# Fixed probability tiles, declared independences and a moved memset in a two-branch attention kernel

## The chip, the core and the metric

The kernel runs on one core of one Trainium2 chip. The metric is the device time of one execution in microseconds (us), as a median of repeated executions. The engines of a core have instruction queues of their own and meet only at semaphores: PE multiplies matrices (PEld is its weight load), DVE reduces and adds, ACT computes exponentials and copies, POOL computes on SBUF tiles, and SP issues most of the DMAs.

## What is computed

The reference runs two attentions over the same input `x` (2048 tokens, 448 features, 16 heads of 28) and mixes them with a gate per token. Branch A looks back over eight positions with a stride of two; branch B is full attention.

```python
g = _sigmoid((x * gate_w).sum(-1, keepdims=True))
# A: logits over idx = pos - 2*[0..7], softmax, weighted sum, @ A_wo
# B: scores = einsum("bhqd,bhkd->bhqk", q, k) * Dh**-0.5
#    o = einsum("bhqk,bhkd->bhqd", softmax(scores), v);  o @ B_wo
return g * a + (1 - g) * b
```

Everything is fp32. Products that need the precision are made of a high and a low part (`QH`, `QL`, `KH`, `KL`), three matmuls for one.

## The kernel before, in words

**Stages.** Up to about 259 us the kernel projects `x` to queries, keys and values; the inputs stand in four pairs of SBUF blocks `xh`, `xl` (pool `xp`, lines 205 and 206) and the results pass through a pool `pp` of eight slots of 4 KB a partition (lines 46 and 86). Then come 256 steps (the loop at line 1034): 16 units `u` (four groups of four heads, by four blocks of 512 queries) by 16 key tiles `kt`. The last twenty or so steps also carry the output projection, and the rest of it follows.

**One step.** `scores` (line 987) issues the matmuls of one key tile in a fixed order of tokens, `WITH` (line 979):

```python
WITH = "10 20 s0 11 21 30 00 12 22 31 01 s1 s2 32 02".split()
```

A token such as `12` is head "1", term 2 of three; heads 1 and 2 share the two banks of `RP[0]` (tile T2), heads 3 and 0 the two banks of `mine`. `s0`, `s1` and `s2` are matmuls of another kind: they compute, for a unit further on, scores whose row maxima are wanted (line 143). `s0` goes to the bank `T1`, `s1` and `s2` to the two banks of `other`. `mine` and `other` are `RP[1]` and `TP` (tiles T0 and T1) and change places each step (line 995).

As soon as `22` is out, ACT takes the exponential of both banks of `RP[0]` (line 1014, "the first exp"), and after `02` that of `mine` ("the second exp"); each writes a tile P of 128 by 1024. DVE takes the maxima of the extra matmuls (line 147): that of `s0` alone, and a second one over `s1` and `s2` together ("the wide reduce", 128x2 from 128x1024). At the end of the step come the eight matmuls of P with the values of the step before (`do_av`, line 973).

The first token of the next step needs `RP[0]` read by the first exp. `s1` needs `other` read by the second exp of the step before. `30` and `00` need `mine`, which was `other` one step earlier, read by the wide reduce of the step before. After step 234 the extra matmuls are finished, and the order `ALONE` (line 980) holds.

**What sets the order.** Each engine's queue is written out by hand: `at` (line 521) hangs a call on a step and a position in it ("pre", "mid", "dve", "act", "end"), and `issue` (line 717) takes the items of branch A from lists by keys, costs and lags in steps. Branch A runs on POOL (multiplications and additions, lines 608 to 663) with its reductions on DVE (line 618). POOL also has a part of finishing each unit: `fin_on` (line 880) multiplies the unit's sum, and ACT (`fin_hi`, line 884) then rounds it, at the position "pre" of a step, ahead of that step's exps in ACT's queue.

**Semaphores.** The framework derives the dependences from the tiles that instructions touch. A tile taken from a pool slot waits for all who used the slot before. Two readers of one PSUM bank on different engines are put in order as well. An instruction carries one wait of its own; where it has more, they stand ahead of it in the queue of its engine as EVENT_SEMAPHORE records. `tc.declare_no_dep` takes a single dependence out. The kernel before uses it only for the banks of the output projection (line 554).

**Memory.** `pp` stays for the whole kernel: its eight slots hold staging tiles in the projection and P afterwards. When the projection ends, `mp` (line 561) takes the space where `xp` lay, with `KH2`, `KL1`, `maskt` and two more; `pm` (line 567, eight tiles of 2 KB for `mtile`) follows. `init_kh(KH[2])` (line 566) sets KH2 to one in POOL's queue, ahead of the memsets of `maskt`; the DMAs that load its keys are issued at step 12 (line 574), and its first use is unit 8.

Of the kernel before, what the change touches and what calls it, by code (L numbers as in the profile page):

```python
# [8 lines left out]
F32 = mybir.dt.float32  # L9
F32R = mybir.dt.float32r  # L10
AF = mybir.ActivationFunctionType
ALU = mybir.AluOpType
X = mybir.AxisListType.X
ET = mybir.EngineType

S, D, H, DH = 2048, 448, 16, 28
# [3 lines left out]
SCALE = DH ** -0.5  # L20
NU = NG * NB
NMX = 192
# [3 lines left out]
def gated_mix_kernel(ctx: ExitStack, tc: tile.TileContext, xT, xn, gw, wA, wB, woAB, out):  # L26
    nc = tc.nc
# [15 lines left out]

    cp = ctx.enter_context(tc.tile_pool(name="cp", bufs=1))
    sp = ctx.enter_context(tc.tile_pool(name="sp", bufs=2))
    pp = ctx.enter_context(tc.tile_pool(name="pp", bufs=8))

# [6 lines left out]
    def banks(n):  # L56
        for i in range(n):
            pool = ctx.enter_context(tc.tile_pool(name=f"t{i}", bufs=1, space=bass.MemoryType.PSUM))
            T.append(pool.tile([128, 2, 512], F32, name=f"T{i}"))
# [12 lines left out]
    KH = [cp.tile([128, S], F32R, name=f"KH{i}") for i in range(2)]  # L72
    KL = [cp.tile([128, S], F32R, name="KL0")]
    MX = cp.tile([128, NMX], F32, name="MX")
# [7 lines left out]
    def init_kh(t):  # L82
        nc.gpsimd.memset(t.bitcast(F32), 1.0)

    def pair(name):
        return pp.tile([128, 2, 512], F32, tag="P", name=name)
# [50 lines left out]
    def s1_mm(n, bank, half=False):  # L137
        u, i = divmod(n, 64)
        qs, kc, h = i // 16, i // 4 % 4, i % 4
        if i == 0 and u + 1 < NU:  # L140
            load_qhi(u + 1)
        r = slice(64 * (h // 2), 64 * (h // 2) + 64) if half else slice(32 * h, 32 * h + DH)
        nc.tensor.matmul(bank, qhis[u][h % 2][r, 128 * qs:128 * qs + 128],  # L143
                         KH[u // NB % 3][r, 512 * kc:512 * kc + 512], start=True, stop=True)

    def s1_max(n, k, bank):
        nc.vector.tensor_reduce(MX[:, n % NMX:n % NMX + k], bank, axis=X, op=ALU.max)  # L147
        if n // 64 != (n + k) // 64:
            finished.append(n // 64)
        s1c[0] = n + k  # L150


    def s1_half(k, half):
# [28 lines left out]
    def max_turn(t):  # L182
        r = sp.tile([128, 32], F32, name="nms")
        nc.vector.transpose(r, t)
        return r
# [18 lines left out]
    with tc.tile_pool(name="xp", bufs=1) as xp, tc.tile_pool(name="wp", bufs=2) as wp:  # L204
# [203 lines left out]
        r, t = xst[:, 0, 0:3, :], xst[:, 0, 3, :]  # L408
# [7 lines left out]
        for kt in range(3):  # L416
            nc.vector.tensor_tensor(out=xl[0][:, kt, :], in0=r[:, kt, :], in1=xh[0][:, kt, :].bitcast(F32),
                                    op=ALU.subtract)
        nc.vector.tensor_tensor(out=tail[64:128], in0=t[64:128], in1=tail[64:128].bitcast(F32), op=ALU.subtract)
        nc.vector.tensor_tensor(out=wl0[:, 3, 0:256], in0=wt0[:, 0:256], in1=wh0[:, 3, 0:256].bitcast(F32),  # L420
                                op=ALU.subtract)
# [27 lines left out]
        for n, t in enumerate(tiles):  # L449
# [4 lines left out]
            for w in splits:  # L454
                i, k = (n - splits[w][0]) * splits[w][1], splits[w][1]
# [44 lines left out]
            if n == 64:  # L500
                gate = []
                for sgn, dst in ((-1.0, g_t), (1.0, omg)):
                    e = sp.tile([128, NJ], F32, name="ez")
# [5 lines left out]
            if n == 70:  # L509
                r = max_turn(omw)  # L510
# [10 lines left out]
    def at(pos, st, f):  # L521
        hooks.setdefault((st, pos), []).append(f)
# [4 lines left out]


    tctx[0].close()
    banks(3)  # L530
    RP = T[2], T[0]
    TP = T[1]
# [28 lines left out]
    mp = ctx.enter_context(tc.tile_pool(name="mp", bufs=1))  # L561


    KH.append(mp.tile([128, S], F32R, name="KH2"))
    KL.append(mp.tile([128, S], F32R, name="KL1"))
    init_kh(KH[2])
    pm = ctx.enter_context(tc.tile_pool(name="pm", bufs=8))

    def mtile(name):
        return pm.tile([128, 512], F32, tag="M", name=name)  # L570

    maskt = mp.tile([128, W, NJ, 2], F32, name="maskt")
    nc.gpsimd.memset(maskt, 0.0)
    for st, g, t, src in ((12, 2, KH[2], qk_hi), (30, 1, KL[1], qk_lo), (72, 2, KL[0], qk_lo),
                          (100, 3, KH[0], qk_hi), (136, 3, KL[1], qk_lo)):
# [107 lines left out]
    for c in range(8):  # L683
# [20 lines left out]
        n = 0  # L704
# [197 lines left out]
    for u in range(NU - 1):  # L902
        f = NJ * (u + 1)
# [76 lines left out]
    ALONE = "10 20 30 00 11 21 31 01 12 22 32 02".split()  # L980
    turn = [0]
    order = []

    def sums(i):
        return pbank[2 if i else 1]

    def scores(u, kt, cur):
        g = u // NB
        n = s1c[0]
        k = min(3, s1e - n)  # L990
        qh, ql = Qs[u]
        ks = slice(128 * kt, 128 * kt + 128)
        mine, other = ((RP[1], TP) if turn[0] == 0 else (TP, RP[1]))
        if k:
            turn[0] = 1 - turn[0]
        bank = {"1": RP[0][:, 0, :], "2": RP[0][:, 1, :], "3": mine[:, 0, :], "0": mine[:, 1, :],
                "s0": T1, "s1": other[:, 0, :], "s2": other[:, 1, :]}
        for tok in WITH if k else ALONE:
            if tok[0] == "s":
                i = int(tok[1])  # L1000
                if i < k:
                    s1_mm(n + i, bank[tok])
                if i == 0:
                    s1_max(n, 1, T1)
                elif i == 2 and k > 1:
                    s1_max(n + 1, k - 1, other[:, 0:k - 1, :])
                continue
            a, t = tok[0], int(tok[1])
            h = (int(a) + n) % 4
            r = slice(32 * h, 32 * h + (DH + 2 if t == 0 else DH))  # L1010
            nc.tensor.matmul(bank[a], (KH[g % 3], KH[g % 3], KL[g % 2])[t][r, ks], (qh, ql, qh)[t][r, :], start=(t == 0), stop=(t == 2))  # L1011
            if t == 2 and a in "20":
                p = pair("P")
                nc.scalar.activation(p, RP[0] if a == "2" else mine, AF.Exp, scale=SCALE)  # L1014
                cur[(h + 3) % 4], cur[h] = p[:, 0, :], p[:, 1, :]
                yield len(cur)

# [16 lines left out]
    for u in range(NU):  # L1034
        g, b = divmod(u, NB)
        for kt in range(NJ):
# [12 lines left out]
            for a in scores(u, kt, cur):  # L1049
                if a == 2:  # L1050
                    run("mid", st)
# [45 lines left out]
    for j in range(12, 16):  # L1097
# [4 lines left out]
        bank = acc[j - 12]  # L1102
# [40 lines left out]
```

## Time and profile before

| | |
|---|---|
| median of 3 executions | 927.08 us (926.46 to 927.43) |
| the profiled execution | 927.55 us; span of its instructions 925.1 us |
| granted TensorE clock | 0.996 |
| PE, DVE, ACT, POOL busy | 914.6, 732.6, 652.8, 620.9 us |
| the 512 exps, line 1014 | 497.1 us, mean 1024 ns |
| the 470 reduces, line 147 | 443.4 us, mean 954 ns |
| first and last reduce of line 147 start at | 260.0 and 797.9 us |

The profile is read thus: a group row gives engine, operation, tiles and count, then busy time, mean time of one, and idle time before with what ended it. A timeline row gives start, time, engine, line, operation, tiles, count, and in brackets how long the engine had been idle and who released it. "PEld T L1011 <- ACT P L1014" in the table of waits reads: the weight load of line 1011 was idle until the ACT instruction of line 1014 released it. PE's times overlap, since matmuls are pipelined and run side by side on separate rows of the array, so that PE counts as busy almost always. A q behind an engine's name (ACTq, DVEq) is its sequencer, where the EVENT_SEMAPHORE records run.

### The profile page before, as it was taken

Reading aid. Unit: us, or ns where it says so; the run is one execution under the profiler, and the core shown is the slowest. Engines: PE = TensorE matmul, PEld = TensorE weight load, DVE = VectorE, ACT = ScalarE, POOL = GpSimd, SP = SyncE. Lnnn points to the kernel's source line nnn. Section 1 sums busy time; section 2 is a strip of 40 time slices with the busy share of each in tenths; the row PEclk is TensorE's granted clock in tenths of the full one; section 3 lists DMA queues with packets and bytes.
Section 4 is the critical chain, followed back from the end, with each engine's and each line's share of the span. In section 5 each row is a group of like instructions: output and inputs, shape, how many; then the busy total and the mean of one; then the engine's idle time right before and its main releaser. Section 6 shows DMA issues by size and latency. Waiting matters only on the chain.

```text
span 925.1 us, 21392 instructions
## 1 busy us (share of the span) xinstructions
PE 914.6 (99%) x8396; PEld 541.3 (59%) x8396; DVE 732.6 (79%) x977; ACT 652.8 (71%) x802; POOL 620.9 (67%) x485
## 2 busy tenths in 40 slices
PE   9899999999999999999999999999999999999998
PEld 6688999999954444444444444444444444466667
DVE  6388999999979999999999999999998888500012
ACT  6346534343378888888888888888989889855551
POOL 2289856464469799999999999999994851300100
PEclk9899999999999999999999999999999999999999
DMA  9867603444362341335135232421412123553422
GB/s 254 283 191 219 185 11 82 130 121 128 104 240 64 99 123 46 88 103 130 41 96 151 85 101 63 139 74 30 107 42 53 33 60 99 149 156 112 137 83 98
DMA packets 101124, 104.34 MB, mean 113 GB/s; under 512 B 61652, under 2 KB 71252, under 8 KB 100240
## 3 DMA queue, kind: packets, MB, share of 16 engines
q1 hardware_dynamic: 100880, 102.72, 39.2%
q8 instruction: 65, 1.06, 0.5%
q10 hardware_dynamic: 144, 0.26, 0.2%
q14 instruction: 35, 0.29, 0.1%
HBM read 61.99 MB, written 40.48 MB: 111 GB/s over the span
## 4 chain that ended last, share of the span: by engine, by line
PE 94%; DMA 2%; ACT 1%; SPq 1%; issue 0%; DVE 0%; POOL 0%; ACTq 0%; DVEq 0%; POOLq 0%
PE T L1011 30%; PE av L973 26%; PE r L296 15%; PE T L812 8%; PE r L291 7%; PE r L143 4%; PE T L143 4%; ACT P L1014 1%; PE T L790 1%; DMA V<-in_xT 1%; DMA onlo<-on_lo 1%; DMA qk_hi<-qkh 0%; DMA KH<-qk_hi 0%; SPq L100 0%; SPq L851 0%
## 5 line engine op out<-in xcount | busy, mean ns | idle before, releaser
L1014 ACT ACTIVATE P<-T 128x1024 f32<-128x1024 f32 x512 | 497.1, 1024 | 89.5 <-PE T L1011 87.6
L147 DVE TENSOR_REDUCE MX<-T 128x1 f32<-128x512 f32 x470 | 443.4, 954 | 39.6 <-PE T L143 15.7
L973 PE MATMUL av<-P,V 128*32 128x512 f32 x2048 | 272.8, 605 | 0.0
L1011 PEld LDWEIGHTS T<-QH,KH 30*128 30x128 f32 x1024 | 90.9, 181 | 228.9 <-ACT P L1014 198.5
L143 PE MATMUL T<-KH,QP 28*128 28x512 f32 x704 | 222.0, 461 | 0.1
L1011 PE MATMUL T<-QH,KH 30*128 30x512 f32 x1024 | 220.6, 491 | 1.4 <-ACT P L1014 1.3
L160 DVE TENSOR_REDUCE MX<-r 128x2 f32<-128x1024 f32 x160 | 192.5, 1221 | 29.4 <-PE r L143 24.7
L1011 PE MATMUL T<-QH,KL 28*128 28x512 f32 x1024 | 189.0, 393 | 0.0
L1011 PE MATMUL T<-QL,KH 28*128 28x512 f32 x1024 | 187.4, 392 | 0.0
L608 POOL TENSOR_TENSOR prod<-qt,kt 128x896 f32<-128x896 f32 x64 | 135.1, 2115 | 4.7 <-DMA kt<-a_scr 4.7
L360 ACT ACTIVATE raw<-r 128x896 f32<-128x896 f32 (+1 forms) x64 | 58.9, 921 | 96.7 <-PE r L296 96.7
L663 POOL TENSOR_TENSOR oat<-oat,prod 128x896 f32<-128x896 f32 x56 | 118.1, 2109 | 2.4
L143 PE MATMUL r<-KH,QP 64*128 64x512 f32 x320 | 99.4, 395 | 3.3 <-DMA KH<-qk_hi 3.2
L143 PEld LDWEIGHTS T<-KH,QP 28*128 28x128 f32 x704 | 86.0, 181 | 23.7 <-ACT P L1014 13.9
L658 POOL TENSOR_TENSOR prod<-vt,L 128x896 f32<-128x896 f32 x56 | 95.5, 1705 | 0.5
L361 POOL TENSOR_TENSOR ast<-raw 128x448 f32<-128x448 f32 x48 | 55.5, 1156 | 57.8 <-ACT raw L360 49.2
L1011 PEld LDWEIGHTS T<-QL,KH 28*128 28x128 f32 x1024 | 92.5, 184 | 0.0
L1011 PEld LDWEIGHTS T<-QH,KL 28*128 28x128 f32 x1024 | 91.8, 183 | 0.9
L296 PE MATMUL r<-wh,xh 64*128 64x448 f32 (+1 forms) x512 | 87.8, 363 | 0.0
L973 PEld LDWEIGHTS av<-P,V 128*32 128x32 f32 x2048 | 40.3, 108 | 78.9 <-issue 73.9
L800 DVE TENSOR_TENSOR oalo<-T,oah 128x384 fp32r<-128x384 f32 x16 | 8.9, 557 | 90.9 <-ACT onhi L799 82.3
L296 PE MATMUL r<-wh,xl 64*128 64x448 f32 (+1 forms) x384 | 70.9, 363 | 0.0
(110 smaller groups left out, 1158.5 us busy)
## 6 DMA issues: line engine op xcount, KB each, us to landing
a_scr<-ast SPq DMA_DIRECT2D x24, 448.0 KB
qk_hi<-qkh SPq DMA_DIRECT2D x24, 256.0 KB
qk_lo<-qkh SPq DMA_DIRECT2D x24, 256.0 KB
rbc<-rs SPq DMA_DIRECT2D x60, 64.0 KB
QP<-qk_hi SPq DMA_DIRECT2D x64, 56.0 KB
KL<-qk_lo SPq DMA_DIRECT2D x16, 224.0 KB
QH<-qk_hi SPq DMA_DIRECT2D x64, 56.0 KB
QL<-qk_lo SPq DMA_DIRECT2D x64, 56.0 KB
```

What stands on the lines that cost most here:

```text
L143: nc.tensor.matmul(bank, qhis[u][h % 2][r, 128 * qs:128 * qs + 128], KH[u // NB % 3][r, 512 * kc:512 * kc + 512], start=True, stop=True)
L147: nc.vector.tensor_reduce(MX[:, n % NMX:n % NMX + k], bank, axis=X, op=ALU.max)
L160: nc.vector.tensor_reduce(m, PM[k], axis=X, op=ALU.max)
L291: nc.tensor.matmul(bank, ws[c][rows, k, t[4]:t[4] + 128], x, start=first, stop=last)
L296: nc.tensor.matmul(bank[:, 0:cols], x, ws[c][rows, k, 0:cols], start=first, stop=last)
L608: nc.gpsimd.tensor_tensor(out=p, in0=qt[c], in1=kvt["k", c % 2][:, HALO - DIL * w:HALO - DIL * w + NJ, :], op=ALU.mult)
L658: nc.gpsimd.tensor_tensor(out=dst.rearrange("p j (h d) -> p j h d", d=DH), in0=kvt["v", c % 2][:, HALO - DIL * w:HALO - DIL * w + NJ, :].r ...
L663: nc.gpsimd.tensor_tensor(out=oat[c], in0=oat[c], in1=oat[c, w], op=ALU.add)
L812: writes(bank, nc.tensor.matmul(bank[:, :D], src, wo[c][:, k, :], start=(first and k == ks[0] and i == 0), stop=(last and k == ks[-1] and ...
L973: nc.tensor.matmul(av[32 * h:32 * h + 32, :], V[:, kt, 4 * g + h, :], tiles_[h], start=(kt == 0), stop=(kt == NJ - 1), skip_group_check=True)
L1011: nc.tensor.matmul(bank[a], (KH[g % 3], KH[g % 3], KL[g % 2])[t][r, ks], (qh, ql, qh)[t][r, :], start=(t == 0), stop=(t == 2))
L1014: nc.scalar.activation(p, RP[0] if a == "2" else mine, AF.Exp, scale=SCALE)
```

## The change

P is no longer taken from the pool `pp` but from eight fixed tiles `probs`, used in turn, in a new pool `ep`. `pp` is closed with the projection; `pm` takes the first half of its space, `KL1` and `KH2` lie in the second half, and the eight tiles come to lie where the `x` blocks lay. The dependence of an exp on the exp that wrote the same tile eight exps earlier is declared away. So is that between successive readers of the two banks that change places: the wide reduce no longer waits for the second exp that read them before it, nor the second exp for the wide reduce. The matmuls that write the tiles or banks in between keep their waits. KH2's memset moves from the start of the attention to the end of step 2 (the third step).

```diff
-    pp = ctx.enter_context(tc.tile_pool(name="pp", bufs=8))
+    pctx = ExitStack()
+    pp = pctx.enter_context(tc.tile_pool(name="pp", bufs=8))
...
     def s1_max(n, k, bank):
-        nc.vector.tensor_reduce(MX[:, n % NMX:n % NMX + k], bank, axis=X, op=ALU.max)
+        r = nc.vector.tensor_reduce(MX[:, n % NMX:n % NMX + k], bank, axis=X, op=ALU.max)
...
+        return r.ins
...
     tctx[0].close()
+    pctx.close()
+    pm = ctx.enter_context(tc.tile_pool(name="pm", bufs=8))
...
+    KL.append(mp.tile([128, S], F32R, name="KL1"))
     KH.append(mp.tile([128, S], F32R, name="KH2"))
-    KL.append(mp.tile([128, S], F32R, name="KL1"))
-    init_kh(KH[2])
-    pm = ctx.enter_context(tc.tile_pool(name="pm", bufs=8))
+    at("end", 2, lambda: init_kh(KH[2]))
...
+    ep = ctx.enter_context(tc.tile_pool(name="ep", bufs=1))
+    probs = [ep.tile([128, 2, 512], F32, name=f"P{i}") for i in range(8)]
...
+    exps = []
+    reader = {}
+
+    def apart(inst, bank):
+        if id(bank) in reader:
+            tc.declare_no_dep(inst, reader[id(bank)], reason="the matmuls between them waited for it")
+        reader[id(bank)] = inst
...
                 elif i == 2 and k > 1:
-                    s1_max(n + 1, k - 1, other[:, 0:k - 1, :])
+                    r = s1_max(n + 1, k - 1, other[:, 0:k - 1, :])
+                    apart(r, other)
...
             if t == 2 and a in "20":
-                p = pair("P")
-                nc.scalar.activation(p, RP[0] if a == "2" else mine, AF.Exp, scale=SCALE)
+                p = probs[len(exps) % 8]
+                e = nc.scalar.activation(p, RP[0] if a == "2" else mine, AF.Exp, scale=SCALE).ins
+                if len(exps) >= 8:
+                    tc.declare_no_dep(e, exps[-8], reason="the matmuls that read it came between")
+                exps.append(e)
+                if a == "0":
+                    apart(e, mine)
```

## The prediction

> **What bounds the kernel now.** I read the page's busy times first, then the table of waits, then the timeline of a few steps in the middle.
>
> ```profile
> span 925.1 us, 21392 instructions
> PE 914.6 (99%) x8396; PEld 541.3 (59%) x8396; DVE 732.6 (79%) x977; ACT 652.8 (71%) x802; POOL 620.9 (67%) x485
> ```
>
> ```profile
> PEld T L1011 <- ACT P L1014: 198.5, 236, 1.1
> ACT P L1014 <- PE T L1011: 87.6, 203, 2.5
> PEld T L1011 <- DVE MX L147: 12.0, 69, 0.5
> POOL prod L608 <- DMA kt<-a_scr: 4.7, 1, 4.7
> POOL L L624 <- DVE L L618: 2.4, 1, 2.4
> ```
>
> PE counts as busy 99% of the span, yet ACT waits for PE at 203 exps and PE's loads wait for ACT at 236 and for DVE at 69. That is a ring in which each waits for the other, and no engine alone sets the pace. To find the ring I follow one chain through three steps, by starts:
>
> ```profile
> 521.18 0.19 PEld L1011 LDWEIGHTS T<-QH,KH 30*128 30x128 f32 x2 [0.84 <-ACT P L1014]
> ...
> 522.25 1.94 ACT L1014 ACTIVATE P<-T 128x1024 f32<-128x1024 f32 x2 [0.41 <-PE T L1011]
> ...
> 524.24 0.18 PEld L143 LDWEIGHTS T<-KH,QP 28*128 28x128 f32 x2 [0.15 <-ACT P L1014]
> ...
> 524.86 1.23 DVE L147 TENSOR_REDUCE MX<-T 128x2 f32<-128x1024 f32 x1 [0.26 <-PE T L1011]
> ...
> 526.13 0.18 PEld L1011 LDWEIGHTS T<-QH,KH 30*128 30x128 f32 x2 [0.15 <-DVE MX L147]
> ...
> 527.03 0.16 PEld L973 LDWEIGHTS av<-P,V 128*32 128x32 f32 x8 [0.36 <-issue]
> ...
> 528.02 0.19 PEld L1011 LDWEIGHTS T<-QH,KH 30*128 30x128 f32 x2 [0.84 <-ACT P L1014]
> ```
>
> A step begins at 521.18. Its two exps start 1.07 later and end at 524.19. That frees `other` for `s1` and `s2` of the next step, loaded at 524.24 (0.05 later). The wide reduce of these starts at 524.86 (0.62) and ends at 526.09 (1.23). This frees the bank of `30` in the step after, loaded at 526.13 (0.04). The matmuls with V follow at 527.03 (0.90), and the next step begins at 528.02 (0.99). The links are 1.07 + 1.94 + 0.05 + 0.62 + 1.23 + 0.04 + 0.90 + 0.99 = 6.84 us for three steps, 2.28 us a step. Over the whole attention:
>
> ```profile
> L147 DVE TENSOR_REDUCE MX<-T x470: 634/699/1229, 260.0 to 797.9; 128x1 f32<-128x512 f32 x79, 128x2 f32<-128x1024 f32 x78
> L147 DVEq EVENT_SEMAPHORE  x234: 21/21/21, 261.0 to 795.6; - x117
> ```
>
> 470 reduces at two a step are 235 steps, so that 234 intervals lie between 260.0 and 797.9: 2.30 us each. The ring of three steps explains 2.28 of 2.30. Two shorter rings lie below it. In one the first exp alone goes back to the next step: 1.07 + 1.02 + 0.05 = 2.14. In the other `s1` leads straight to the V matmuls (the second exp's end at 524.19 lets `s1` load at 524.24, and the first row below shows 0.45 from there): (1.07 + 1.94 + 0.05 + 0.45 + 0.99) / 2 = 2.25.
>
> ```profile
> 524.69 0.16 PEld L973 LDWEIGHTS av<-P,V 128*32 128x32 f32 x8 [0.26 <-issue]
> ```
>
> **The waits declared away.** The row of 234 DVE records above, one for each wide reduce but one, and the row of ACT below show how the second wait is paid for:
>
> ```profile
> L1014 ACTq EVENT_SEMAPHORE  x490: 17/17/924, 259.5 to 894.9; - x164
> L1014 ACT ACTIVATE P<-T x512: 1013/1024/1068, 260.5 to 895.8; 128x1024 f32<-128x1024 f32 x171
> ```
>
> 490 records stand before 512 exps. By the code the first exp has two waits, the matmul `22` and the exp that used its P slot before; so has the second, `02` and the wide reduce before it; and so has the wide reduce, `s2` and the exp before it. In each pair the second wait is old by the time the first ends, but the instruction leaves its queue only after the record. What a record costs is seen in the tail of the attention, where some exps have none. Both of these steps have the same matmuls in front:
>
> ```profile
> 836.54 0.51 PE L1011 MATMUL T<-QH,KH 30*128 30x512 f32 x4
> ...
> 837.55 1.94 ACT L1014 ACTIVATE P<-T 128x1024 f32<-128x1024 f32 x2 [0.97 <-PE T L1011]
> ...
> 850.97 0.51 PE L1011 MATMUL T<-QH,KH 30*128 30x512 f32 x4
> ...
> 852.05 1.94 ACT L1014 ACTIVATE P<-T 128x1024 f32<-128x1024 f32 x2 [2.53 <-PE T L1011]
> ```
>
> ```profile
> L1014 ACTq EVENT_SEMAPHORE  x2: 17/17/17, 852.0 to 852.1; - x2
> ```
>
> The last row is line 1014 in the window 850.5 to 853; in 836.5 to 839 there is no such row. From the first matmul to the exp it is 1.01 us without the record and 1.08 with it: 0.07 us, or 0.017 if only the record's own time counted. I take 0.065. The second exp's record runs under the first exp and costs nothing as long as the exps follow each other (1.94 for both in the rows above); its going gains nothing. For DVE I compare the reduce of `s0`, which has a single wait, with the wide one:
>
> ```profile
> 523.34 0.49 PE L143 MATMUL T<-KH,QP 28*128 28x512 f32 x1
> ...
> 523.91 0.69 DVE L147 TENSOR_REDUCE MX<-T 128x1 f32<-128x512 f32 x1 [0.17 <-PE T L143]
> ...
> 524.24 0.50 PE L143 MATMUL T<-KH,QP 28*128 28x512 f32 x2
> ```
>
> The first matmul ends at 523.83 and its reduce starts 0.08 later; the pair ends at 524.74 and the wide reduce starts 0.12 later. The record costs 0.04 by this, 0.021 by its own time, and as much as on ACT (0.07) at most. I take 0.04. No lengthening is possible from the removal itself, since each instruction keeps the wait that ends last.
>
> Each of the two lies once in the ring of three steps: (0.065 + 0.04) / 3 = 0.035 us a step, which leaves 2.245, as the ring through `s1` goes down by 0.065 / 2 to 2.22 and stays below. Times 234 steps: 8.2 us. By the ends it is (0.017 + 0.021) / 3 x 234 = 3.0 us and (0.07 + 0.07) / 3 x 234 = 10.9 us. In the steps of the tail PE works on the output projection while the exps wait (0.97 and 2.53 us above); nothing is gained there.
>
> The Trainium skill speaks against the DVE half. "VectorE: DVE Perf Modes", in the sections "The DRAIN you can't avoid" and "Rules for kernel authors", says that between chained DVE operations the semaphores cost nothing and only the number of operations counts. By this rule the 0.04 would be zero; no run here yet separates the two.
>
> **What a faster step meets: POOL.** From the end of branch A's start-up to its last unit:
>
> ```profile
> 311.20:703.00 391.80, 391.60 (x3927) 161.81 (x3923) 371.75 (x562) 343.89 (x386) 382.65 (x257) 1.00 0.32 86
> ```
>
> ```profile
> POOL nmt L179 <- ACT nmv L178: 5.3, 3, 4.1
> POOL finv L842 <- DVE finv L841: 1.0, 2, 0.6
> POOL lr L646 <- DVE lr L642: 1.0, 2, 0.6
> ```
>
> ```profile
> 475.35 1.29 POOL L880 TENSOR_TENSOR on<-osb,rbc 128x512 f32<-128x512 f32 x1
> ...
> 478.09 0.63 ACT L884 ACTIVATE onhi<-on 128x512 fp32r<-128x512 f32 x1
> ```
>
> In these 391.8 us (171 steps of 2.29) POOL is busy 382.65, and all that it waits is 1.0 + 1.0 + 5.3, of which 4.1 lies at the edge: 3.2 us. POOL's work doesn't shrink. Its instructions are bound to steps, so that POOL falls behind PE by what PE gains there, 171 x 0.035 = 6.0 us, less the 3.2 that it needn't idle any more: 2.8 us. Behind it stands ACT's rounding of `on`, at the head of a step and ahead of its exps. In the pair above it starts 1.45 us after POOL is done (475.35 + 1.29 = 476.64). Once POOL is that late, ACT waits, and PE behind it. So the window can give 3.2 + 1.45 = 4.65 rather than 6.0, and I take 1.3 us off. The 63 steps outside give their 2.2 us. Net: 6.9 us.
>
> **Tiles and memory.** ACT never waited for POOL or a DMA at line 1014 (its wait by far is the 87.6 for PE), so P's old slots cost no time and the new place gains none. The first exps then overwrite blocks that projection matmuls read, and PE runs those ahead of the exp's own matmul. I cost it at zero.
>
> **KH2's fill.**
>
> ```profile
> L83 POOL MEMSET KH<- x3: 1805/1805/1812, 1.3 to 261.6; 128x2048 f32 x3
> ```
>
> The memset, 1.8 us from 261.6, is covered by POOL's idle 4.7 us before its first product, which waits for a DMA. Moved behind step 2 it still comes ahead of that product, but waits for the last staging tiles in its new place. Late by the whole 1.8 us it would move branch A's start; then the 2.4 us that POOL idles at line 624 take it up. Its loads at step 12 on SP come much later. Zero either way.
>
> **Rivals.** (1) *Only the exp's record matters*, as the skill's rule has it: 0.065 / 3 x 234 = 5.1 us, 3.7 of it in POOL's window, below 4.65, so all of it stays: 922.0. For it: the DVE difference is 0.04 us between matmuls whose ends are modelled. Against it: DVE waits for PE there in most steps, so the record lies behind the wait. (2) *POOL holds the window entirely*: it is late from the start, none of its idle time or slack is to be had, and only the 63 steps outside gain 2.2 us: 924.9. For it: 382.65 of 391.8. Against: the 1.45 us is measured. (3) *The change doesn't remove the records*: the tiles bring another second wait, or the framework joins the dependences otherwise. No change, 927. (4) *Slower*: exps that write P in its new place take longer. Both lie one after the other in the ring, so x longer costs 2x / 3 in each of 234 steps, 156x. It eats the 6.9 us at x = 0.044 and makes the kernel slower by 0.2% from x = 0.056; with x = 0.07 it gives 931. Against it: over all eight old slots the exps take 1013 to 1068 ns with a median of 1024, so that the place of a tile shows little.
>
> **How the numbers follow.** The sum is made on the profiled execution: 927.55 - 6.9 = 920.65. The median shown is 0.47 below it, so I forecast 927.08 - 6.9 = 920.2. Chances: forecast 0.62, (1) 0.15, (2) 0.10, (3) 0.08, (4) 0.05. The range takes in (1) and the bounds of the record's cost: at the lower end 3.0 us, all inside POOL's allowance, 924.1; at the upper end 10.9 us where POOL's lag costs little, about 917.0 after 0.8 us of it. About 0.2% (1.9 us, 925.2) is what a measurement here can tell from no change. Forecast, (1) and (2) are faster by more: 0.87; (3) is the same, 0.08; (4) slower, 0.05.
>
> **What would show it.** Right: line 1014 and the wide reduce have almost no EVENT_SEMAPHORE records; the reduces of line 147 cover about 8 us less from first to last; from a step's first load to its exp there are 1.00 to 1.01 us instead of 1.07; POOL's waits between 311 and 703 shrink, and ACT shows waits of some tenths at line 884 for line 880. Steps in the tail keep their length. Wrong: the records are there; or they are gone and the interval stays at 2.30; or the exps are longer than 1024 ns; or DVE's line 618 or ACT's line 884 waits for POOL by several us.

## The result and the profile after

The changed kernel takes 919.14 us (median of 5, 918.6 to 920.1) against 927.08 before (median of 5, 926.46 to 929.9). The ratio is 0.9908 with a 95% interval of 0.9895 to 0.9921: 7.9 us less, faster by more than the 0.2% that can be told. The profiled execution took 918.6 us with a span of 916.7 us.

First the groups of line 148 (147 before) and of line 1027 (1014 before) in the changed kernel: count, minimum, median and maximum in ns, first and last start in us.

```profile
L148 DVE TENSOR_REDUCE MX<-T x470: 631/699/1235, 258.8 to 789.5; 128x1 f32<-128x512 f32 x79, 128x2 f32<-128x1024 f32 x78
L148 DVEq EVENT_SEMAPHORE  x1: 21/21/21, 259.8 to 259.8; - x1
```

```profile
L1027 ACT ACTIVATE P<-T x512: 1007/1024/1149, 259.2 to 887.3; 128x1024 f32<-128x1024 f32 x171
L1027 ACTq EVENT_SEMAPHORE  x3: 17/17/17, 258.3 to 262.1; - x3
```

The records are gone: 1 instead of 234 at the reduces, 3 instead of 490 at the exps. The work itself takes as long as before (medians 699 and 1024 ns). The reduces now cover 530.7 us from first to last instead of 537.9. So 7.2 us of the 8.4 by which the spans differ come from the attention; 1.2 us lie ahead of it, since the first reduce starts at 258.8 instead of 260.0. That part isn't the change's: in the other runs of the changed code the first reduce starts between 258.6 and 261.0 us, with the same code ahead of it (the last section says what goes with this). From the last reduce to the end of the span it is 127.2 us in both kernels, so that the tail is as long as before.

The chain through three steps, in the timeline of the changed kernel:

```profile
482.43 0.18 PEld L1024 LDWEIGHTS T<-QH,KH 30*128 30x128 f32 x2 [0.84 <-ACT P L1027]
...
483.45 1.94 ACT L1027 ACTIVATE P<-T 128x1024 f32<-128x1024 f32 x2 [0.38 <-PE T L1024]
...
485.44 0.18 PEld L144 LDWEIGHTS T<-KH,QP 28*128 28x128 f32 x2 [0.18 <-ACT P L1027]
...
485.99 1.22 DVE L148 TENSOR_REDUCE MX<-T 128x2 f32<-128x1024 f32 x1 [0.15 <-PE T L1024]
...
487.26 0.18 PEld L1024 LDWEIGHTS T<-QH,KH 30*128 30x128 f32 x2
...
488.17 0.16 PEld L978 LDWEIGHTS av<-P,V 128*32 128x32 f32 x8 [0.37 <-issue]
...
489.17 0.18 PEld L1024 LDWEIGHTS T<-QH,KH 30*128 30x128 f32 x2 [0.84 <-ACT P L1027]
```

1.02 + 1.94 + 0.05 + 0.55 + 1.22 + 0.05 + 0.91 + 1.00 = 6.74 us for three steps, 2.25 a step. Two links are shorter than before: from the first load to the exp 1.02 instead of 1.07, from the load of `s1` to the wide reduce 0.55 instead of 0.62. The load of `30` has no bracket any more, because PEld stood idle for only 0.09 us before it and waits under 0.15 us aren't listed. It still starts 0.05 us after the wide reduce ends, here and in 225 of the 227 steps from 6 to 232, so the ring is closed as before.

Two steps are clearly longer than before: from first load to first load step 79 takes 2.93 us (2.17 before), step 159 takes 3.38 (2.36). Their rows in the changed kernel:

```profile
439.55 0.49 PE L1024 MATMUL T<-QH,KH 30*128 30x512 f32 x2 [0.74 <-DMA QH<-nm]
```

```profile
618.24 1.30 POOL L885 TENSOR_TENSOR on<-osb,rbc 128x512 f32<-128x512 f32 x1
...
619.58 0.63 ACT L889 ACTIVATE onhi<-on 128x512 fp32r<-128x512 f32 x1 [1.03 <-POOL on L885]
```

The first matmul of step 80 waits 0.74 us for the queries of the new unit. In step 159 ACT waits 1.03 us for POOL's product, with that step's exps behind it. Before, neither wait existed. The last two DMAs of those queries were issued at these times, in the kernel before and in the changed one:

```profile
439.73 1.07 SPq L100 DMA_DIRECT2D QH<-nm  x2
```

```profile
436.96 1.07 SPq L101 DMA_DIRECT2D QH<-nm  x2
```

Step 79 begins at 440.92 before, 1.19 us after that issue, and at 436.59 in the changed kernel, 0.37 us ahead of it.

### The profile page after: what moved, and what is told of

It reads as the page before. It is cut to its first block, busy times and chain, and to the rows that moved or that the text cites. A ratio compares the mean times of both kernels' runs of the same rounds, so it can differ in the third digit from the quotient of the medians.

```text
span 916.7 us, 20680 instructions
## 1 busy us (share of the span) xinstructions
PE 904.7 (99%) x8396; PEld 539.3 (59%) x8396; DVE 731.4 (80%) x977; ACT 652.1 (71%) x802; POOL 620.9 (68%) x485
## 4 chain that ended last, share of the span: by engine, by line
PE 80%; POOL 11%; DMA 3%; SPq 2%; ACT 2%; issue 1%; DVE 0%; POOLq 0%; ACTq 0%; DVEq 0%
PE T L1024 22%; PE av L978 20%; PE r L298 15%; PE T L817 8%; PE r L293 7%; PE r L144 4%; POOL prod L613 3%; POOL oat L668 3%; PE T L144 3%; POOL prod L663 2%; SPq L101 2%; ACT P L1027 1%; PE T L795 1%; DMA KL<-qk_lo 1%; DMA V<-in_xT 1%
## 5 line engine op out<-in xcount | busy, mean ns | idle before, releaser
L1027 ACT ACTIVATE P<-T 128x1024 f32<-128x1024 f32 x512 | 497.4, 1025 | 81.0 <-PE T L1024 79.6
L144 PE MATMUL T<-KH,QP 28*128 28x512 f32 x704 | 219.6, 454 | 0.1
L1024 PE MATMUL T<-QH,KH 30*128 30x512 f32 x1024 | 211.2, 489 | 3.0 <-ACT P L1027 2.0
L1024 PE MATMUL T<-QH,KL 28*128 28x512 f32 x1024 | 185.7, 395 | 0.0
L1024 PE MATMUL T<-QL,KH 28*128 28x512 f32 x1024 | 183.5, 392 | 0.0
```

Of the source, the lines that this page charges most:

```text
L1027: e = nc.scalar.activation(p, RP[0] if a == "2" else mine, AF.Exp, scale=SCALE).ins
```

## The experiments

All are edits of the changed kernel, compared with the kernel before on the same chip. Since the start of the attention shifts by some 2 us from run to run, the column "reduces" gives the time from the first to the last start of the reduce's group, as above.

| run | median us | ratio to before (95%) | reduces us |
|---|---|---|---|
| before | 927.08 | | 537.9 |
| the change | 919.14 | 0.9908 (0.9895 to 0.9921) | 530.7 |
| e1_tiles_only | 927.17 | 0.9995 (0.9981 to 1.0009) | 537.8 |
| e2_exp_only | 922.15 | 0.9936 (0.9917 to 0.9955) | 533.6 |
| e3_reduce_only | 922.16 | 0.9941 (0.9920 to 0.9963) | 533.2 |
| e4_second_exp_keeps | 920.22 | 0.9917 (0.9898 to 0.9936) | 530.5 |
| e5_both_eased | 920.18 | 0.9918 (0.9901 to 0.9935) | 530.5 |
| e6_hi_later | 920.49 | 0.9926 (0.9907 to 0.9945) | 530.6 |
| e7_q_earlier | 918.99 | 0.9909 (0.9890 to 0.9928) | 530.6 |
| e8_on_q_earlier | 918.04 | 0.9909 (0.9895 to 0.9923) | 529.6 |
| e9_on_earlier | 918.49 | 0.9919 (0.9899 to 0.9938) | 529.4 |

**The tiles alone.** No dependence is declared away.

```diff
     def apart(inst, bank):
-        if id(bank) in reader:
-            tc.declare_no_dep(inst, reader[id(bank)], reason="the matmuls between them waited for it")
         reader[id(bank)] = inst
...
-                if len(exps) >= 8:
-                    tc.declare_no_dep(e, exps[-8], reason="the matmuls that read it came between")
                 exps.append(e)
```

> The eight fixed tiles, the pools and KH2's fill as in the changed kernel, with no dependence declared away, so every second wait is back. Theory (the second waits were paid on the ring exp, exp, s1, wide reduce): no gain, 927.1 within 0.7 us, 1.07 us from a step's first load to its exp, 234 records at the wide reduce. Rival (the tiles' place or the moved fill brings it): 919 to 920, with the records there.

The groups of its line 148 and 1025:

```profile
L148 DVE TENSOR_REDUCE MX<-T x470: 636/698/1231, 258.9 to 796.7; 128x1 f32<-128x512 f32 x79, 128x2 f32<-128x1024 f32 x78
L148 DVEq EVENT_SEMAPHORE  x234: 21/21/21, 259.9 to 794.4; - x117
```

```profile
L1025 ACTq EVENT_SEMAPHORE  x493: 17/17/17, 258.4 to 893.8; - x165
```

The records are back and so is the time, 537.8 us against 537.9. The place of the tiles, the pools and KH2's fill gain and cost nothing together.

**The exps' wait alone.** The body of `apart` is left out as in e1; the declaration against the exp eight before stays.

> Of the three kinds of wait only that of an exp on the exp eight before is declared away; the wide reduce keeps its wait for the exp, and the second exp its wait for the reduce. Theory: 0.06 us less in the ring of three steps, 0.02 a step over 234 steps, 4.7 us less: 922.4 (921.5 to 923.5). Rival (only the exp's record counts, that of DVE costs nothing): about 919.1, all of the gain.

```profile
L148 DVE TENSOR_REDUCE MX<-T x470: 631/698/1233, 259.9 to 793.5; 128x1 f32<-128x512 f32 x79, 128x2 f32<-128x1024 f32 x78
L148 DVEq EVENT_SEMAPHORE  x234: 21/21/21, 260.9 to 791.2; - x117
```

```profile
L1025 ACTq EVENT_SEMAPHORE  x226: 17/17/17, 259.4 to 793.2; - x113
```

The reduces' records are all there; of the 493 at the exps 226 are left. The attention is 4.2 us shorter than with the tiles alone. The rival, which gave all of the gain to this half, falls.

**The wide reduce's wait alone.**

```diff
     def apart(inst, bank):
-        if id(bank) in reader:
+        if id(bank) in reader and inst.engine == ET.DVE:
...
-                if len(exps) >= 8:
-                    tc.declare_no_dep(e, exps[-8], reason="the matmuls that read it came between")
```

> Only the wide reduce's wait for the exp is declared away; both exps keep theirs. Theory: with 0.04 us in the ring 3.1 us less, 924.0; with 0.065, as the changed trace has it from s1's load to the wide reduce (0.55 for 0.61), 5.1 us less, 922.0. Rival (no cost of semaphores between DVE operations): 927.1.

```profile
L148 DVE TENSOR_REDUCE MX<-T x470: 633/702/1234, 260.0 to 793.2; 128x1 f32<-128x512 f32 x79, 128x2 f32<-128x1024 f32 x78
L148 DVEq EVENT_SEMAPHORE  x1: 21/21/21, 261.1 to 261.1; - x1
```

4.6 us shorter than with the tiles alone. The record in front of a DVE instruction does cost time; the higher of the two expectations fits, 0.065 us rather than 0.04. The links of the ring show the two halves apart. These are medians over steps 5 to 232 or 233, in us:

| link | before | e2 | e3 | the change |
|---|---|---|---|---|
| first load to first exp | 1.075 | 1.015 | 1.074 | 1.013 |
| end of the second exp to the wide reduce of the next step | 0.664 | 0.674 | 0.596 | 0.598 |

Each half shortens its own link by about 0.06 us and leaves the other nearly as it was. In the trace of the kernel before, the record of the wide reduce that starts at 524.86 runs from 524.79 to 524.81, just behind the matmuls, and waits for the same semaphore as the reduce of `s0`, that of PE. So the wait that ends last stands in the record and the old one on the instruction, and the reduce starts 0.065 us after its record. Whether the other order would be free wasn't tried. Not all of e3's 4.6 us are of this kind: 0.4 come from step 137 (2.70 us in e1, 2.29 in e3), where the wide reduce of the step before starts late. In the kernel before, its engine is idle for 0.27 us there, with "issue" as the releaser; why is open.

**The second exp keeps its wait.** Only the first line of e3's edit.

> All as in the changed kernel, but the second exp keeps its wait for the wide reduce. Theory: its record runs under the first exp, so nothing changes: 919.1 within 0.7 us. Rival (the second exp's record is on the path too): some 2 to 5 us longer, 921 to 924.

```profile
L1027 ACTq EVENT_SEMAPHORE  x226: 17/17/17, 258.1 to 788.7; - x113
```

226 records stand before the second exps, and the reduces cover 530.5 us, the change's 530.7. A record under a running exp costs nothing. The median of the whole runs, 920.22 us, is 1.1 above the change's, but the intervals overlap.

**Where the rest of the two halves went.** 4.2 + 4.6 = 8.8 us, but together they gave 7.1 (537.8 to 530.7). Steps 79 and 159, longer by 0.76 and 1.02 us, make up as much as is missing. The next runs take away their two waits.

```diff
-            u, (1, 3, 6, 8, 12, 15, 16, 19))
+            u, (1, 3, 6, 8, 12, 16, 16, 19))
...
-            if kt == 12 and u + 1 < NU:
+            if kt == (12 if u == NU - 2 else 11) and u + 1 < NU:
                 load_q(u + 1)
```

> The changed kernel, with the unit's rounding on ACT one step later (position 16 instead of 15 behind the unit) and the queries of the next unit loaded one step earlier (step 11 instead of 12, but for the last unit). Theory (the gains of the two records add up to 10 us or so in the attention, and two new waits eat the rest: ACT for POOL in step 159, 1.0 us, PE for the DMA of QH at step 80, 0.7 us): both waits go, steps 79 and 159 fall to 2.1 to 2.4 us, 1.7 us less than the changed kernel, 917.4. Rival (the two halves overlap in the ring and don't add): 919.1, with another wait in their place or none.

> Only the rounding on ACT one step later. Theory: step 159 falls from 3.4 to about 2.35 us and ACT no longer waits for POOL; the wait for QH at step 80 stays: 1.0 us less than the changed kernel, 918.1. Rival (ACT's wait hides behind others): step 159 keeps its length.

> Only the load of the queries one step earlier. Theory: step 79 falls from 2.9 to about 2.2 us, the wait of PE for the DMA of QH goes, step 159 stays at 3.4: 0.7 us less than the changed kernel, 918.4. POOL's lag is then less made up by that halt, so ACT may wait for POOL a little more. Rival (the DMA is held by SP's queue, which is no faster from an earlier step): the wait stays.

e6 has only the first edit, e7 only the second. None of the three has a shorter attention: 530.5, 530.6 and 530.6 us. In e5 and e6 ACT no longer waits for POOL, and PE no longer for QH; in e6 the latter was not expected. There step 79 begins 0.6 us later, counted from the attention's first load (179.07 against 178.43 us). Steps 79 and 159 fall by 1.9 us together, yet 1.7 are paid in other steps. ACT's timeline of e5 in step 128 shows how:

```profile
550.65 0.22 ACT L179 ACTIVATE nmt<-m 128x16 fp32r<-128x16 f32 x1
550.77 0.20 ACT L180 ACTIVATE nmv<-m 128x16 f32<-128x16 f32 x1
550.88 0.61 ACT L889 ACTIVATE onhi<-on 128x512 fp32r<-128x512 f32 x1
551.40 1.92 ACT L1027 ACTIVATE P<-T 128x1024 f32<-128x1024 f32 x2
...
552.45 0.18 PEld L1024 LDWEIGHTS T<-QH,KH 30*128 30x128 f32 x2 [1.03 <-ACT P L1027]
```

One step later the rounding meets two other copies, the exp starts late, and the next step begins 0.2 us late (1.03 against 0.84 of idle weight load). Only step 128 was followed like this; what the other steps pay for isn't shown. In e7 the wait for QH goes, but PE's lead over POOL is then larger (the rounding of the product begun in step 94 follows 0.03 us behind it, 0.56 in the changed kernel), and ACT's wait in step 159 grows from 1.0 to 1.3 us. Of the 0.79 us that step 79 falls by, 0.25 are lost in step 159 and about 0.4 in small amounts between steps 80 and 144. My expectation of 1.7, 1.0 and 0.7 us failed: shifting a wait on the side that waits isn't the same as having POOL earlier.

**POOL's product earlier.** ACT's rounding stays, and POOL's product moves ahead by a step. e9 has the edit below alone, e8 also loads the queries earlier as e7 does.

```diff
-            u, (1, 3, 6, 8, 12, 15, 16, 19))
+            u, (1, 3, 6, 8, 11, 15, 16, 19))
```

> The changed kernel with POOL's product of the unit one step earlier in POOL's queue (position 11 instead of 12), ACT's rounding left where it was, and the queries loaded one step earlier. Theory (the two waits cost what they last, and moving ACT's rounding into the next step only cost the same again in other places, at steps 48, 128 and 192): nothing is moved on ACT, both waits go, and the reduces of line 148 cover 530.7 - 1.7 = 529.0 us; 917.4. Rival (POOL holds the attention, and what is eased in one place is paid in another): they cover 530.7 still, with waits for POOL elsewhere.

> Only POOL's product one step earlier. Theory: step 159 falls from 3.4 to about 2.3, step 79 stays at 2.9; the reduces of line 148 cover 529.7 us. Rival (POOL holds): 530.7.

The groups of line 148 in e8 and in e9:

```profile
L148 DVE TENSOR_REDUCE MX<-T x470: 669/694/1230, 258.9 to 788.5; 128x1 f32<-128x512 f32 x79, 128x2 f32<-128x1024 f32 x78
```

```profile
L148 DVE TENSOR_REDUCE MX<-T x470: 669/693/1229, 260.1 to 789.5; 128x1 f32<-128x512 f32 x79, 128x2 f32<-128x1024 f32 x78
```

529.6 and 529.4 us, 1.1 and 1.3 less than the change, by one trace each. In both traces ACT waits for POOL nowhere in the attention, nor PE for QH. That e9 alone ends the wait for QH, which I hadn't expected, is told by SP's waits between 405 and 440 us, in the changed kernel and in e9:

```profile
SPq L851 <- POOL finv L847: 8.7, 1, 8.7
```

```profile
SPq L851 <- POOL finv L847: 6.8, 1, 6.8
```

SP's queue stands at the unit's DMA until POOL has made its input, and the loads of the next unit's queries stand behind it. POOL's lag so reaches PE by two ways, through ACT and through SP's queue. With POOL's work in another order SP stands 1.9 us less, and in e9 the queries' last two DMAs go out 1.36 us ahead of step 79, which begins at 438.12:

```profile
436.76 1.07 SPq L101 DMA_DIRECT2D QH<-nm  x2
```

Part of what e8 and e9 win they lose again in step 225, which takes 2.76 and 2.63 us against 2.28 in the changed kernel. In both ACT makes two copies there ahead of the exps, in e8 at:

```profile
766.81 0.58 ACT L760 ACTIVATE wo<-wor 128x448 fp32r<-128x448 f32 x1
767.28 0.60 ACT L833 ACTIVATE osb<-av 128x512 f32<-128x512 f32 x1
```

In the changed kernel ACT makes only the second of them in that step; the first copy of line 760 follows at 772.73, two steps later.

e8 has the lowest median of all, 918.04 us, but its interval and the change's overlap; the gain over the change is seen in the attention's own time alone.

## Why the prediction was right, point by point

**The ring.** The forecast left 2.245 us a step; the three steps shown take 2.247, but they are three without a new wait: the average over 234 steps is 2.265 (2.296 before; the forecast's 2.30 runs from a reduce of `s0` to a wide one and so takes in a little more than 234 steps). The reduces cover 7.2 us less, where 6.9 were forecast. This nearness is in part luck, since the errors of three terms below, 0.9 too much, 1.5 too little and 0.4 too little taken off, nearly cancel. The total, 919.14 where 920.2 was forecast, also has the earlier start of the attention in it.

**The exps' record.** The forecast put 5.1 us on it; e2 measured 4.2, which is 0.054 us a ring. **The wide reduce's record.** It put 0.04 us a ring on it, 3.1 us; e3 measured 4.6, so 4.6 x 3 / 234 = 0.059 us a ring, or 0.054 without the 0.4 us of step 137, the same as on ACT. This term was too small; I had read the difference off the modelled ends of matmuls. By both terms the sum was 8.2, measured 8.8. It isn't (0.062 + 0.066) / 3 x 234 = 10.0, as the two shortened links would have it, so not every step can lie on this ring. Rival (1) falls: e3 by itself gains 0.6%, with an interval of 0.2% on either side. The Trainium skill's rule in "VectorE: DVE Perf Modes" ("The DRAIN you can't avoid"), that semaphores between DVE operations cost nothing, doesn't hold here for a wait for another engine that stands ahead in the queue.

**The second exp's record** was costed at nothing; e4 shows 530.5 us against 530.7. **The tail** was forecast to keep its length, and it does (127.2 us). **The tiles and KH2's fill** were costed at nothing; e1 shows 0.1 us. POOL's timeline of the changed kernel shows the cover that was named:

```profile
264.82 1.80 POOL L84 MEMSET KH<- 128x2048 f32 x1
268.01 2.11 POOL L613 TENSOR_TENSOR prod<-qt,kt 128x896 f32<-128x896 f32 x1 [1.39 <-DMA kt<-a_scr]
```

The fill now stands in front of the first product, and of POOL's 4.7 us of idle time before it 1.39 are left.

**POOL.** The forecast took off 1.3 us because POOL would fall behind and ACT would wait for it at the rounding. POOL did fall behind: from the end of its product to the rounding it was 1.45, 2.20, 1.95 and 1.88 us for the products begun in steps 94, 109, 125 and 157 before, and it is 0.56, 0.75, 0.32 and 0.03 for the same units in the changed kernel. The pair that gave 1.45 was one of the closest. The wait appeared there, but in one step with 1.03 us, where several of some tenths were forecast; the missing part of the two halves is 8.8 - 7.1 = 1.7 us, of which 1.1 to 1.3 come back when POOL's product is made a step earlier. What it missed is the second way, through SP's queue to the load of the queries (0.74 us at step 80). The steps 23 to 192, which lie in POOL's window, gain 4.8 us and the others 2.4, where 4.65 and 2.2 were forecast; in e9, with both waits gone, the window gains 6.35, and 6.0 were forecast for it without POOL. Rival (2), in which nothing is to be had in POOL's window, falls: e8 and the change both gain there. Of the 0.4 to 0.6 us that remain, step 225 has 0.48 in e8 and 0.35 in e9; the last tenth is open.

**Rivals (3) and (4)** fall with the counts of records (3 and 1) and the exps' median of 1024 ns in their new place.

## What to carry to other kernels

In a kernel whose engines wait for each other in a ring, look for instructions with two waits: the second, long since fulfilled, may cost 0.06 us each time the first ends late, and it was free at the second exp, which waits behind the first on its own engine (e4). Multiply by how often the ring passes it, not by how often it stands in the program. Then see which engine that did not gain is full, and which queues stand behind it: a queue that waits for it holds back transfers that have nothing to do with it.

## What the runs showed that I had not expected

A wait that was taken away from one side came back on another: with the rounding one step later (e6), steps 79 and 159 won 1.9 us and other steps lost 1.7, the most in steps 128 and 129 with 0.2 each (530.6 against 530.7 us). And the start of the attention differs by 2.4 us between runs whose code ahead of it is the same (first reduce from 258.6 to 261.0 us), more than several of the effects measured here. It goes with the granted TensorE clock early in the projection. The five traces that start by 259.1 show 0.93 between 23 and 46 us and 1.00 between 46 and 70; the six that start at 259.9 or later, that of the kernel before among them, show 0.87 to 0.90 and 0.96 to 0.99. What lowers the clock there isn't shown. The span of the attention alone is steadier: 530.5, 530.5, 530.6, 530.6 and 530.7 us in the changed kernel and four edits of it that don't shorten it, and 537.9 and 537.8 in the kernel before and e1.
